# A convolution and two MLP layers on one core: the second product goes tile by tile in three banks, with the low parts of two chunks added up

## The chip, the cores and the metric

One NeuronCore of a Trainium2 chip runs the kernel; the other cores are idle. The metric is the device time of one execution in microseconds (us), lower is better. Three runs of the kernel before gave 2135.5, 2136.12 and 2136.22 us, median 2136.12.

## What is computed

Three stages follow each other on 16384 tokens of width 192, all in float32:

```
w   = softmax(weight, axis=-1)              # 8 heads x 7 taps
y   = causal convolution of x over 7 tokens, head h (24 columns) with taps w[h]
h   = y @ w_in1   (192 -> 2048);  g = max(h, 0)**2;       z   = g @ w_out1   (2048 -> 192)
h   = z @ w_in2   (192 -> 2048);  g = max(0.01*h, h);     out = g @ w_out2   (2048 -> 192)
```

The products run on TensorE in float32r, one pass each. To keep float32 accuracy every operand is split into a high part (rounded to float32r) and a low part (the rest), and three products are added: high by high, high weight by low data, low weight by high data.

## The kernel before, in words

**Tiles.** Tokens go in 32 tiles of 512 (`NT`, `TT`). The hidden width 2048 goes in 16 chunks of 128 (`NF`), two chunks to a step index p from 0 to 7 (`NP`). A *unit* is a tile in one of the two layers, l = 1 or 2; in what follows (l, t) names it. Two tiles make a pair q.

**Half arrays.** Every matmul uses 64 of the 128 rows of the array (`halves(0)` or `halves(1)`), and two of them, one on each half, run side by side. Such a couple is called a *slot* here. [...]

**First product.** `g1(u, p)` makes the two chunks of step p for one tile: 9 slots, into two of four banks `h`. Each item that this generator yields is one slot.

**Between the products.** ScalarE takes a chunk out of its bank with a ReLU (layer 1, line 531) or a leaky ReLU (layer 2, line 533) into `g`; in layer 1 it is squared, one chunk on ScalarE (line 540), the other on VectorE (line 538). `high` (line 558, ScalarE) rounds `g` to `hi`; `low` (line 562, VectorE) makes `lo = g - hi`. The tiles `g`, `hi` and `lo` come from pools of 4, 5 and 5 buffers.

**Second product.** `g2(u, f)` takes chunk f of both tiles of a pair: 10 slots, into four banks: `o0m` and `o1m` (128 output columns of each tile) and `o0r` and `o1r` (the 64 others; high by high and low weight by high data lie side by side in one matmul and are added later). In its middle the halves change banks. The change is guarded by a GpSimd no-op that waits for the last matmul of one half, and for which the first matmul of the other half waits; two slots of the next `g1` stand between (`AHEAD = 2`).

**Order of work.** A step of the main loop is one tile and one p: the tiles of a pair alternate, so a pair has 16 steps, and the phases are pairs 0 and 1 in layer 1, pairs 0 and 1 in layer 2, pairs 2 and 3 in layer 1, and so on. A step issues `g1` of its own chunks and `g2` of two steps before (`LAG = 2`), 9 + 10 = 19 slots. At the end of a pair `evac` (lines 694 to 703) empties the four banks before the next pair's second product begins, five slots of `g1` further on (`GAP = 5`). In the first 16 steps a hand-written table (`ROW`) orders ScalarE and VectorE, since the weights are decoded there; later a budget of VectorE time per step (`STEP = 4100`, in ns) decides how many *pieces* are put between: taps of the convolution (line 390), 32x32 transposes (lines 366, 720), splits of the next operand (lines 430, 439), decoding of the weights.

**Four phases of 16 steps** make the steady cycle: one pair of a layer has 16 steps, two pairs per layer, two layers.

Of the kernel before, what the change touches and what calls it, by code (L numbers as in the profile page):

```python
# [20 lines left out]
STEP = 4100  # L21
DEBT = -4000
# [4 lines left out]
SECOND, THIRD = 16, 40  # L27
LEAD_W = 2
# [3 lines left out]
XB = 4  # L32
# [17 lines left out]
    "ybpdwLAyBdpapwThrp",  # L50
    "ldppABabhlp",
    "AyBydpabhdww",
    "lyAdappLhplBdwp",
    "pAbpapyhBprbywd",
# [6 lines left out]
def conv_moe_moe2_kernel(  # L61
# [46 lines left out]
    NM = NI + 2 * P  # L108
    W, WR = {}, {}

    def place(l, p):
        if (l, p) not in W:
            z = const.tile([P, 2 * NW], F32R, tag=f"w{l}{p}", name=f"w{l}")
            W[l, p] = z[:, 0:2 * NM].rearrange("p (a w) -> p a w", a=2)
            WR[l, p] = z[:, 2 * NM:].rearrange("p (c w) -> p c w", c=2)
        return W[l, p], WR[l, p]

    def lent(p, dtype=I32):

        return const.tile([P, 2 * NW], dtype, tag=f"w2{p}", name="lent")  # L120
# [3 lines left out]

    def weights_in(l, v, p, a, k):
        return W[l, p][v, a, P * k:P * k + P]

    def weights_out(l, v, f, what):
        p, c = divmod(f, 2)
        z, n = W[l, p][v], NI + P * c  # L130
        if what in ("m", "ml"):
            return z[:, len(what) - 1, n:n + P]
        return WR[l, p][v, c, 0:2 * R if what == "r" else R]
# [6 lines left out]
    ring, turns = const.tile([P, 3, TT], F32, name="ring"), [0]  # L140

    def ring_tile():
        turns[0] += 1
        return ring[:, turns[0] % 3, :]

    def load_w(l, p, t):

        t4 = t[:, 0:NI].rearrange("p (k f) w -> p k (f w)", k=3)
# [6 lines left out]
        for c0, d0, n in ((NI, 0, P), (NM, P, R)):  # L155
            nc.sync.dma_start(  # L156
                out=t[:, c0:c0 + 2 * n].rearrange("p (c d) w -> p c (d w)", d=n), in_=src[:, :, 2 * d0:2 * (d0 + n)]
            )
# [18 lines left out]
    def decode(l, p, t, a, b):  # L177
# [4 lines left out]
        e = min(b, NM)  # L182
        z, r = place(l, p)
        parts = [(lambda z: z[:, 0:e - a], z[:, 0, a:e], z[:, 1, a:e])]
        if b == NW:
            parts.append((lambda z: z[:, NM - a:n].rearrange("p (c d) -> p c d", d=R), r[:, :, 0:R], r[:, :, R:2 * R]))
# [41 lines left out]

        def copy_high():
            for of, high, _ in parts:  # L230
                nc.scalar.copy(out=high, in_=f32(of(T["t"])))
            ready[l, p, 0] = True

        def sign():
# [4 lines left out]
            if l == 1 and p >= BY_DMA:  # L239
                for of, high, _ in parts:  # L240
                    nc.sync.dma_start(out=f32(high), in_=f32(of(T["t"])))
                ready[l, p, 0] = True
            else:
# [8 lines left out]
        def low_():  # L252
            assert not by_add or "added" in T
            ready[l, p, 1] = True
            for of, _, low in parts:
                nc.vector.scalar_tensor_tensor(  # L256
                    out=low, in0=of(T["r"]) if by_add else f32(of(lo_w)), scalar=2.0 ** -20, in1=f32(of(T["p"])), op0=ALU.mult, op1=ALU.mult
                )

        return [(one, mantissa), (two, rest)], [(one, exponent)], [(two, sign), (one, power), (two, low_)]  # L260


# [4 lines left out]
    def room(u):  # L267

        if len(order) < XB:
            return True  # L270
        return u in X or g1_left[order[len(order) - XB]] == 0

# [277 lines left out]
    def late_chunk(u, f):  # L550
        return u in [(2, t) for t in ordered] and f > NF - 4
# [12 lines left out]
    final = {}  # L564
    in_turn = mybir.DependencyInfo(mybir.DependencyClass.Sync, mybir.DependencyReason.DATA)

    def g2(u, f):
# [3 lines left out]
        if f == 0:  # L571
            ops[u] = {(i, n): ps_o.tile([P, TT], F32, tag=f"o{i}{n}", name=f"o{i}{n}") for i in range(2) for n in "mr"}
# [7 lines left out]
        for part in range(2):  # L580
            side = part ^ (f % 2)
            for j, (n, c, z) in enumerate(main + rest):
                begin = f == 0 and part == 0 and j in (0, 3)
                end_ = f == NF - 1 and part == 1 and j in (2, 4)
                for half in range(2):
# [5 lines left out]
                    final[i, n] = ins  # L591
# [7 lines left out]

    def g2_last(u):  # L600


        l, q = u
        o = ops[u]
        F = range(NF - 4, NF)
        a = {(i, f): hi.pop(((l, 2 * q + i), f)) for i in range(2) for f in F}
        b = {(i, f): lo.pop(((l, 2 * q + i), f)) for i in range(2) for f in F}

        def of(i, n, chunks, closing=False):
            for f in chunks:  # L610
                kinds = [("m", a), ("ml", a), ("m", b)] if n == "m" else [("r", a), ("rh", b)]
                if closing and f == F[-1]:
                    kinds.reverse()
                for c, z in kinds:
                    yield i, n, f, c, z[i, f]

        plan = [
            [of(0, "r", F[:2]), of(1, "r", F[:2]), of(0, "r", F[2:]), of(1, "m", F[:1]), of(1, "r", F[2:]), of(1, "m", F[1:]),
             of(0, "m", F)],
            [of(1, "m", F[:1]), of(0, "m", F), of(0, "r", F, True), of(1, "r", F, True), of(1, "m", F[1:])],  # L620
        ]
        side = (NF - 5) % 2 ^ 1
        owner = {}
        for half in range(2):
            owner[side ^ half, "m"] = owner[1 - (side ^ half), "r"] = half
        by = {k: final.get(k) for k in owner}
        seq = [[x for y in z for x in y] for z in plan]
        left = {k: sum(x[:2] == k for z in seq for x in z) for k in owner}
        for pair in zip(*seq):
            for half, (i, n, f, c, z) in enumerate(pair):  # L630
                k = i, n
                left[k] -= 1
                rows = R if c == "rh" else P
                v = halves(half)
                ins = product(o[k][0:rows], weights_out(l, v, f, c), z[v], False, left[k] == 0).ins
                if owner[k] != half:
                    done = nc.gpsimd.nop(nofuse=True).ins
                    tc.add_manual_dep(done, by[k].name, in_turn, reason="halves take turns on a bank")
                    tc.add_manual_dep(ins, done.name, in_turn, reason="halves take turns on a bank")
                owner[k], by[k] = half, ins  # L640

    def evac_last(u):
        l, q = u
        o = ops.pop(u)
        z = ring_tile()
        t = f32(stage.tile([P, NW], I32, tag="m", name="zs")[:, 0:TT])
        y = stage.tile([P, 3, TT], F32, tag="w", name="y", bufs=2)
        dmas = [nc.sync, nc.scalar]

        def store(j, n, d0, i):  # L650
            r0 = (2 * q + i) * TT
            dmas[j % 2].dma_start(
                out=out[r0:r0 + TT, d0:d0 + 32].rearrange("(i t) d -> t i d", t=32),
                in_=y[32 * j:32 * j + 32, n].rearrange("p (i d) -> p i d", d=32),
            )

        for i in range(2):
            nc.scalar.copy(out=t[halves(i)], in_=o[i, "r"][halves(1 - i)])
        for i in range(2):
            v = halves(i)  # L660
            nc.vector.tensor_add(out=z[v], in0=o[i, "r"][v], in1=t[v])
            nc.vector.transpose(out=y[v, 2], in_=z[v])
            for j in range(2):
                store(2 * i + j, 2, P + 32 * j, i)
        nc.vector.transpose(out=y[:, 0], in_=o[0, "m"])
        c = f32(spare_tile())
        turned = [ps_h.tile([P, 2, P], F32, tag="h", name="turned") for _ in range(2)]
        for i in range(2):
            tokens = slice(2 * P * i, 2 * P * (i + 1))
            nc.scalar.copy(out=c[:, tokens], in_=o[1, "m"][:, tokens])  # L670
            for k in range(2):
                w = c[:, P * (2 * i + k):P * (2 * i + k + 1)]
                nc.tensor.matmul(out=turned[i][:, k, :], lhsT=w, rhs=ident, start=True, stop=True)
        for j in range(4):
            store(j, 0, 32 * j, 0)
        for i in range(2):
            w = y[:, 1, 2 * P * i:2 * P * (i + 1)]
            nc.vector.tensor_copy(out=w, in_=turned[i].rearrange("p k d -> p (k d)"))
            r0 = (2 * q + 1) * TT + 2 * P * i
            dmas[i].dma_start(  # L680
                out=out[r0:r0 + 2 * P, 0:P].rearrange("(k t) d -> t k d", t=P),
                in_=w.rearrange("p (k d) -> p k d", d=P),
            )

    def evac(u):

        l, q = u
        o = ops.pop(u)
        T = [2 * q, 2 * q + 1]
        z = {}  # L690

        def take(i):
            z[i] = ring_tile()
            (nc.vector.tensor_copy if i else nc.scalar.copy)(out=z[i], in_=o[i, "m"])

        def shift(i):
            if i == 0:
                z["s"], z["r"] = f32(stage.tile([P, NW], I32, tag="m", name="zs")[:, 0:TT]), ring_tile()
# [16 lines left out]
        y = {}  # L715

        def turn(n, src):
            if not y:
# [426 lines left out]
```

## Time and profile before

| what | value |
|---|---|
| median of the runs | 2136.12 us |
| span of the profiled execution | 2134.3 us (the runs' median lies 1.8 us above it) |
| TensorE busy | 2126.8 us, 100% of the span, 19512 matmul records |
| VectorE busy | 1328.9 us, 62% |
| ScalarE busy | 1417.1 us, 66% |
| GpSimd busy | 12.4 us, 1% |
| granted TensorE clock | 0.9 or more of full speed in all 40 slices |

How to read it: TensorE is never idle for long after the start, so what counts on it is the number of slots and the time of one. The busy shares of VectorE and ScalarE are means over two layers of different load. An engine that is idle a third of the time still sets when an operand is ready, because each engine runs its queue in order.

### The profile page before, as it was taken

Reading aid. Unit: us, or ns where it says so; the run is one execution under the profiler, and the core shown is the slowest. Engines: PE = TensorE matmul, PEld = TensorE weight load, DVE = VectorE, ACT = ScalarE, POOL = GpSimd, SP = SyncE. Lnnn points to the kernel's source line nnn. Section 1 sums busy time; section 2 is a strip of 40 time slices with the busy share of each in tenths; the row PEclk is TensorE's granted clock in tenths of the full one; section 3 lists DMA queues with packets and bytes.
Section 4 is the critical chain, followed back from the end, with each engine's and each line's share of the span. In section 5 each row is a group of like instructions: output and inputs, shape, how many; then the busy total and the mean of one; then the engine's idle time right before and its main releaser. Section 6 shows DMA issues by size and latency. Waiting matters only on the chain.

```text
span 2134.3 us, 46985 instructions
## 1 busy us (share of the span) xinstructions
PE 2126.8 (100%) x19512; PEld 2042.4 (96%) x19512; DVE 1328.9 (62%) x2083; ACT 1417.1 (66%) x2599; POOL 12.4 (1%) x34
## 2 busy tenths in 40 slices
PE   9999999999999999999999999999999999999999
PEld 6999999999999999999999999999999999999998
DVE  8986686546865368653686536954468544685433
ACT  7986567655676557765577655776557765577654
POOL 1000000000000000000000000000000000000000
PEclk9999999999999999999999999999999999999999
DMA  8631133011330112301223002231023210321101
GB/s 192 160 90 36 14 56 61 18 36 16 56 66 11 36 29 44 74 11 26 43 32 72 16 21 46 34 68 26 11 48 50 49 36 3 59 45 32 31 5 27
DMA packets 233005, 95.06 MB, mean 45 GB/s; under 512 B 204184, under 2 KB 219032, under 8 KB 232792
## 3 DMA queue, kind: packets, MB, share of 16 engines
q1 hardware_dynamic: 227512, 88.70, 21.2%
q0 software_dynamic: 1168, 2.75, 0.7%
q8 instruction: 152, 2.49, 0.5%
q10 hardware_dynamic: 4112, 0.62, 0.2%
q14 instruction: 61, 0.50, 0.1%
HBM read 25.19 MB, written 12.58 MB: 18 GB/s over the span
## 4 chain that ended last, share of the span: by engine, by line
PE 97%; DVE 1%; DMA 1%; SPq 0%; ACT 0%; issue 0%; ACTq 0%; DVEq 0%
PE h L499 46%; PE o1m L499 15%; PE o0m L499 15%; PE o0r L499 10%; PE o1r L499 10%; DMA raw_a<-in_x_dram 0%; DVE lo L562 0%; DVE acc_b L390 0%; DMA w_all<-in_weight_dram 0%; DVE w L256 0%; SPq L346 0%; SPq L156 0%; DMA raw_b<-in_x_dram 0%; DVE x L435 0%; ACT hi L558 0%
## 5 line engine op out<-in xcount | busy, mean ns | idle before, releaser
L499 PE MATMUL h<-x,w 64*128 64x512 f32 x9216 | 1216.4, 376 | 0.5 <-DVE x L435 0.5
L562 DVE TENSOR_TENSOR lo<-g,hi 128x512 fp32r<-128x512 f32 x1018 | 675.4, 689 | 748.0 <-ACT hi L558 664.6
L499 PEld LDWEIGHTS h<-x,w 64*128 64x128 f32 x9216 | 1021.0, 186 | 28.7 <-DVE x L435 0.9
L558 ACT CAST hi<-g 128x512 fp32r<-128x512 f32 x1016 | 600.0, 616 | 26.1 <-DVE g L538 17.5
L499 PE MATMUL o1m<-hi,w 64*128 64x512 f32 x2036 | 602.9, 376 | 0.0
L499 PE MATMUL o0m<-hi,w 64*128 64x512 f32 x2036 | 602.5, 376 | 0.0
L533 ACT ACTIVATE g<-h 128x512 f32<-128x512 f32 x512 | 305.6, 597 | 420.7 <-PE h L499 418.5
L531 ACT ACTIVATE g<-h 128x512 f32<-128x512 f32 x512 | 302.9, 594 | 227.9 <-PE h L499 227.3
L499 PE MATMUL o1m<-lo,w 64*128 64x512 f32 x1018 | 383.3, 376 | 1.0 <-DVE lo L562 0.9
L499 PE MATMUL o1r<-hi,w 64*128 64x512 f32 x1018 | 383.2, 376 | 0.0
L499 PE MATMUL o0m<-lo,w 64*128 64x512 f32 x1018 | 382.9, 376 | 0.0
L499 PE MATMUL o0r<-hi,w 64*128 64x512 f32 x1018 | 382.8, 376 | 0.0
L499 PE MATMUL o1r<-lo,w 64*64 64x512 f32 x1018 | 382.8, 376 | 0.0
L499 PE MATMUL o0r<-lo,w 64*64 64x512 f32 x1018 | 382.8, 376 | 0.0
L499 PEld LDWEIGHTS o0m<-hi,w 64*128 64x128 f32 x2036 | 354.9, 185 | 19.5
L499 PEld LDWEIGHTS o1m<-hi,w 64*128 64x128 f32 x2036 | 354.8, 185 | 19.6
L499 PEld LDWEIGHTS o1m<-lo,w 64*128 64x128 f32 x1018 | 189.3, 186 | 2.6 <-DVE lo L562 2.6
L499 PEld LDWEIGHTS o1r<-hi,w 64*128 64x128 f32 x1018 | 189.3, 186 | 1.0 <-issue 0.2
L499 PEld LDWEIGHTS o0r<-hi,w 64*128 64x128 f32 x1018 | 189.3, 186 | 0.8
L499 PEld LDWEIGHTS o0m<-lo,w 64*128 64x128 f32 x1018 | 189.3, 186 | 0.2
L540 ACT ACTIVATE g<-g 128x512 f32<-128x512 f32 x269 | 168.2, 628 | 0.2
L538 DVE TENSOR_TENSOR g<-g 128x512 f32<-128x512 f32 x243 | 166.4, 685 | 0.5
(115 smaller groups left out, 1065.5 us busy)
## 6 DMA issues: line engine op xcount, KB each, us to landing
x<-x SPq DMA_DIRECT2D x189, 256.0 KB
out_dram<-y SPq DMA_DIRECT2D x184, 64.0 KB
raw_a<-in_x_dram SPq DMA_DIRECT2D x127, 64.0 KB
raw_b<-in_x_dram SPq DMA_DIRECT2D x62, 64.0 KB
lent<-in_moe_w_out_dram SPq DMA_DIRECT2D x13, 256.0 KB
lent<-in_moe_w_in_dram SPq DMA_DIRECT2D x13, 192.0 KB
lent<-in_moe_w_in_dram SPq DMA_DIRECT2D x13, 128.0 KB
lent<-in_moe_w_out_dram SPq DMA_DIRECT2D x13, 128.0 KB
```

The source lines that it names most:

```text
L499: return nc.tensor.matmul(out=o.rearrange("p (b a) -> p b a", a=2), lhsT=w, rhs=z.rearrange("p (a b) -> p b a", a=2), start=begin, stop=end_,)
L531: nc.scalar.activation(out=g, in_=hps.pop((u, f)), func=ACTF.Relu)
L533: nc.scalar.activation(out=g, in_=hps.pop((u, f)), func=ACTF.Prelu, alpha=0.01)
L538: nc.vector.tensor_mul(out=g, in0=g, in1=g)
L540: nc.scalar.activation(out=g, in_=g, func=ACTF.Square)
L558: nc.scalar.copy(out=a, in_=gsp[u, f])
L562: nc.vector.tensor_sub(out=b, in0=gsp.pop((u, f)), in1=f32(hi[u, f]))
```

## The change

The second product now takes one tile at a time, in **three banks**, and all 16 chunks of a tile are done before the next tile begins. Units go one by one, (1,t), (1,t+1), (2,t), (2,t+1), eight steps each; only pair 0 still runs as a pair. So tile changes come every 8 steps. A step still has `g1` of its own chunks (9 slots), now cut in 5 + 2 + 2, and the second product of the step before the last, in three groups of three slots (`g2_one`, `paired`, `COVER = 2`), one after each cut. The three banks of a tile are called M, F and E below, as in `evac_one`: M holds 128 columns by half the array, F and E the others, and E is finished after the second group of the last step, M and F after the third. Four bank tags are handed round, so a new tile has one bank free and takes over E, then F, then (one tile on) M.

From step 48 on (`THREE = 48`) VectorE also **adds the low parts** of the two chunks of a step (`add_low`, line 619 of the changed file, tile `both`), and GpSimd makes **differences of weight columns** (`differences`: one copy and two subtractions, 128x64 each, per layer and p, once) such that one matmul with `both` and two with a single low part and a difference take the place of matmuls on each low part: 9 slots instead of 10. Emptying a tile (`evac_one`): `early` copies E twice (ScalarE, lines 743, 744), `other` copies a half of F (ScalarE, 747), `add_rest` reads F (VectorE, 750), `add_main` reads M (VectorE, 753). `SHORT = 3880` replaces `STEP` in the budget from step 48 on. The weights lie in another layout, for which GpSimd copies two blocks of 64 columns per layer and p (`repeats`). Operand tiles go from four buffers to three.

The core of the diff (the layout of the weights, the last unit, stores and the table are left out):

```diff
-XB = 4
+XB = 3
+THREE = 48
+COVER = 2
...
+    def differences(l, p):
+        z = W[l, p]
+        nc.gpsimd.tensor_copy(out=z[:, BH1:BH1 + R], in_=f32(z[:, A1 + R:A1 + P]))
+        for to, x, y in ((DA, A1, AH0), (DC, CH0, CH1)):
+            nc.gpsimd.tensor_tensor(out=z[:, to:to + R], in0=f32(z[:, x:x + R]), in1=f32(z[:, y:y + R]), op=ALU.subtract)
...
+    def add_low(u, p):
...
+        nc.vector.tensor_add(out=c, in0=f32(lo[u, 2 * p]), in1=f32(lo[u, 2 * p + 1]))
...
+    def chain_of(u, p):
...
+        G, L = (2, 1) if t % 2 == 0 else (1, 2)
+        of = {0: [("m", 0, a[0]), ("m", 1, a[1])], G: [("g", 0, a[0]), ("g", 1, a[1])], L: [("l", 0, a[0]), ("l", 1, a[1])]}
+        if c is not None:
+            of[G].append(("d", 0, b[0]))
+            of[0].append(("d", 1, b[1]))
+            of[L].append(("s", 0, c))
+        else:
+            of[0] += [("m", 0, b[0]), ("m", 1, b[1])]
+            of[L][1:1] = [("rh", 0, b[0]), ("rh", 1, b[1])]
...
+    def g2_one(u, p):
+        if p == 0:
+            ops[u] = [new_bank() for _ in range(3)]
+        of = chain_of(u, p)
+        turn = ((0, 1, 2), (1, 2, 0)) if p % 2 == 0 else ((2, 1, 0), (0, 2, 1))
...
+            else:
+                z = g2_one(u2, p2)
+                advance(going, going[1] - 2 * COVER)
+                run(z, 1)
+                advance(going, COVER)
+                run(z, 1)
+                advance(going)
+                run(z)
+                if p2 == NP - 1:
+                    alone = True
+                    leaving, then = evac_one(u2)
...
+                one, two = (Z, A) if l == 1 else (A, Z)
+                act(*one)
+                act(*two)
+                needed(s, 10000)
+                if not (alone and dec):
+                    pieces(s, left, 700)
+                if l == 1:
+                    square(*Z, vector)
+                    square(*A, False)
+                if alone:
+                    leaving[1]()
+                    leaving[2]()
+                pieces(s, left)
...
+                high(*one)
+                high(*two)
+                low(*one)
+                low(*two)
+                if three:
+                    add_low(u, p)
+                if alone:
+                    leaving[3]()
```

**TensorE's queue.** In the steady part of the kernel before, layer 1, half of a step's second product and the slots around it (`h` is the first product, `w_...` a weight buffer; a row with x4 stands for four matmuls, two slots):

```order
L499 MATMUL o1m<-hi,w_222 128x512 [waits Pool_sequencer_49]
L499 MATMUL o0m<-hi,w_222 128x512
L499 MATMUL o1m<-hi,w_222 128x512
L499 MATMUL o0m<-hi,w_222 128x512
L499 MATMUL o1m<-lo,w_222 128x512
L499 MATMUL o0m<-lo,w_222 128x512
L499 MATMUL o0r<-hi,w_222 128x512
L499 MATMUL o1r<-hi,w_222 128x512
L499 MATMUL o0r<-lo,w_222 64x512
L499 MATMUL o1r<-lo,w_222 64x512
L499 MATMUL h<-x,w_251 128x512 x4
```

And the first two groups of a tile's first step in the changed kernel, in layer 1; `o0r` is the bank E and `o1m` the bank F of the tile before:

```order
L544 MATMUL o0r<-hi,w_222 128x512 [waits PE_49,Activation_49]
L544 MATMUL o1r<-hi,w_222 128x512
L544 MATMUL o0r<-hi,w_222 128x512
L544 MATMUL o1r<-lo,w_222 128x512 [waits DVE_49]
L544 MATMUL o0r<-lo,w_222 128x512 [waits DVE_49]
L544 MATMUL h<-x,w_311 128x512 x4
L544 MATMUL o0r<-hi,w_222 128x512 [waits Pool_sequencer_49]
L544 MATMUL o1m<-hi,w_222 128x512 [waits DVE_49]
L544 MATMUL o0r<-hi,w_222 128x512
L544 MATMUL o1m<-hi,w_222 128x512
L544 MATMUL o0r<-lo,w_222 128x512
L544 MATMUL o1m<-both,w_222 128x512
```

Ten matmuls between two pieces of `g1` have become six, twice there is a hand-over through GpSimd in a step instead of once, and the second group waits for VectorE's `add_rest`. In all 10240 matmuls into the banks `o` have become 9312.

**VectorE's queue**, two steps of layer 1 with a tile change, before (`g<-g` is the square, 390 a tap, 694 to 703 `evac`, 720 a transpose of the output):

```order
L562 TENSOR_TENSOR lo<-g,hi 128x512 [waits PE_49,Activation_49] x2
L694 COPY ring<-o1m 128x512 [waits PE_49]
L703 TENSOR_TENSOR ring<-o0r,zs 64x512 [waits Activation_49]
L703 TENSOR_TENSOR ring<-o1r,zs 64x512 [waits Activation_49]
L538 TENSOR_TENSOR g<-g 128x512
L720 STREAM_TRANSPOSE y<-ring 128x512
L562 TENSOR_TENSOR lo<-g,hi 128x512 [waits Activation_49] x2
L538 TENSOR_TENSOR g<-g 128x512 [waits Activation_49]
```

and in the changed kernel, the second and third step of (1,t) with t even (583 is the square, 607 `low`, 435 a tap, 763 a transpose of the output):

```order
L435 SCALAR_TENSOR_TENSOR acc_b<-xT_b,taps,acc_b 128x512
L583 TENSOR_TENSOR g<-g 128x512 [waits Activation_49]
L750 TENSOR_TENSOR ring<-o0r,zs 64x512 [waits Activation_49]
L435 SCALAR_TENSOR_TENSOR acc_b<-xT_b,taps,acc_b 128x512 [waits DVE_49] x2
L607 TENSOR_TENSOR lo<-g,hi 128x512 [waits Activation_49] x2
L619 TENSOR_TENSOR both<-lo 128x512 [waits DVE_49]
L753 TENSOR_TENSOR ring<-o1r,ring 128x512
L763 STREAM_TRANSPOSE y<-ring 128x512 [waits DVE_49]
L583 TENSOR_TENSOR g<-g 128x512 [waits Activation_49]
L607 TENSOR_TENSOR lo<-g,hi 128x512 [waits Activation_49]
L607 TENSOR_TENSOR lo<-g,hi 128x512 [waits PE_49,Activation_49]
L619 TENSOR_TENSOR both<-lo 128x512 [waits DVE_49]
```

The square, the two low parts and the sum of a step now stand in one run at its end, and the square of the same step stands before its own low parts; before, the two chunks of a step were one step apart.

## Rows read from the trace of the kernel before

**Rows 1.** The page, part 1: busy time of each engine.

```profile
span 2134.3 us, 46985 instructions
...
PE 2126.8 (100%) x19512; PEld 2042.4 (96%) x19512; DVE 1328.9 (62%) x2083; ACT 1417.1 (66%) x2599; POOL 12.4 (1%) x34
```

**Rows 2.** Busy time by stretch: two of the start, then layer 1, layer 2.

```profile
core 0: us, PE busy (x) PEld busy (x) DVE busy (x) ACT busy (x) POOL busy (x), PEclk, DMA share, GB/s
18.66:98.80 80.14, 78.67 (x666) 69.01 (x667) 75.69 (x122) 72.55 (x127) 8.11 (x9) 1.00 0.84 197
98.80:164.46 65.66, 65.66 (x611) 62.67 (x609) 58.93 (x88) 54.62 (x100) 0.00 (x0) 1.00 0.28 73
...
820.62:951.85 131.23, 131.23 (x1220) 127.26 (x1218) 85.90 (x134) 95.44 (x174) 0.00 (x0) 1.00 0.19 35
951.85:1083.08 131.23, 131.23 (x1219) 127.25 (x1218) 73.41 (x118) 76.48 (x144) 0.00 (x0) 1.00 0.22 39
```

**Rows 3.** The chain that ended last: start us, us; two pair changes.

```profile
820.62 2.59 PE h L499 x24
886.24 2.59 PE h L499 x24
```

**Rows 4.** Groups by form: busy us, mean ns | idle before.

```profile
L562 DVE TENSOR_TENSOR lo<-g,hi 128x512 fp32r<-128x512 f32 x1018 | 675.4, 689 | 748.0 <-ACT hi L558 664.6 <-PE o1r L499 48.9 <-PE o0r L499 32.1
...
L885 POOL MEMSET idle<- 128x512 f32 x1 | 0.5, 525 | 0.0
```

**Rows 5.** Timeline of TensorE at a hand-over of banks: start us, us.

```profile
1003.27 0.38 PE L499 MATMUL o0r<-lo,w 64*64 64x512 f32 x1
1003.43 0.65 PE L499 MATMUL h<-x,w 64*128 64x512 f32 x4
...
1003.75 0.18 PEld L499 LDWEIGHTS o1m<-hi,w 64*128 64x128 f32 x1
...
1003.86 0.38 PE L499 MATMUL o1m<-hi,w 64*128 64x512 f32 x1
```

**Rows 6.** Timeline of VectorE in layer 1: start us, us, [idle before].

```profile
822.62 0.69 DVE L703 TENSOR_TENSOR ring<-o1r,zs 64x512 f32<-64x512 f32 x1
823.35 0.69 DVE L538 TENSOR_TENSOR g<-g 128x512 f32<-128x512 f32 x1
...
824.72 0.69 DVE L562 TENSOR_TENSOR lo<-g,hi 128x512 fp32r<-128x512 f32 x1
...
830.96 0.16 DVE L365 COPY xT_a<-xT_a 128x6 f32<-128x6 f32 x1
831.16 0.71 DVE L366 STREAM_TRANSPOSE xT_a<-raw_a 128x512 f32<-128x512 f32 x1
831.79 0.67 DVE L720 STREAM_TRANSPOSE y<-ring 128x512 f32<-128x512 f32 x1
...
832.75 1.29 DVE L562 TENSOR_TENSOR lo<-g,hi 128x512 fp32r<-128x512 f32 x2
833.95 0.68 DVE L538 TENSOR_TENSOR g<-g 128x512 f32<-128x512 f32 x1
834.55 2.32 DVE L390 SCALAR_TENSOR_TENSOR acc_a<-xT_a,taps,acc_a 128x512 f32<-128x512 f32 x3
836.79 1.29 DVE L562 TENSOR_TENSOR lo<-g,hi 128x512 fp32r<-128x512 f32 x2
```

**Rows 7.** Timeline of ScalarE in layer 1: start us, us, [idle before].

```profile
821.29 0.58 ACT L699 COPY zs<-o0r 64x512 f32<-64x512 f32 x1
821.90 0.58 ACT L699 COPY zs<-o1r 64x512 f32<-64x512 f32 x1
822.50 0.60 ACT L531 ACTIVATE g<-h 128x512 f32<-128x512 f32 x1
824.07 0.62 ACT L558 CAST hi<-g 128x512 fp32r<-128x512 f32 x1 [0.98 <-DVE g L538]
824.60 0.62 ACT L540 ACTIVATE g<-g 128x512 f32<-128x512 f32 x1
...
838.51 0.60 ACT L531 ACTIVATE g<-h 128x512 f32<-128x512 f32 x1 [1.32 <-PE h L499]
839.01 0.61 ACT L558 CAST hi<-g 128x512 fp32r<-128x512 f32 x1
```

**Rows 8.** Waits: who waited for whom: us in total, times, longest.

```profile
POOL ring L209 <- DVE g L538: 9.5, 1, 9.5
```

**Rows 9.** Timeline of the end: last matmul into a bank, last VectorE instruction.

```profile
2128.20 0.38 PE L499 MATMUL o1m<-spare,w 64*128 64x512 f32 x1
...
2130.47 0.87 DVE L678 COPY y<-turned 128x256 f32<-128x256 f32 x2 [1.01 <-PE turned L673]
```

More of the change, by code (lines that the diff above doesn't have):

```diff
@@ L227, in exponent, with made @@
             on_scalar(lambda: nc.scalar.activation(out=T["t"], in_=T["t"], func=ACTF.Relu, scale=8.0, bias=bias_e))
+        def made(what):
+            T[what] = True
+            if a == 0 and "low" in T and "high" in T:
+                repeats(l, p)
         def copy_high():
-            for of, high, _ in parts:
-                nc.scalar.copy(out=high, in_=f32(of(T["t"])))
+            for of, to in highs:
+                nc.scalar.copy(out=to, in_=f32(of(T["t"])))
             ready[l, p, 0] = True
+            made("high")
         def sign():
@@ L597, in g2 @@
             yield
-    def g2_last(u):
[L603 to L640, printed above, removed]
@@ new lines, in paired @@
+    def paired(u, seqs, fresh, closing):
+        l, t = u
+        o = [z for z, _ in ops[u]]
+        left = {k: sum(x[0] == k for z in seqs for x in z) for k in range(3)}
+        used, start = {}, 0
+        assert len(seqs[0]) == len(seqs[1])
+        for j, pair in enumerate(zip(*seqs)):
+            assert pair[0][0] != pair[1][0]
+            if any(used.get((pair[h][0], 1 - h), -9) >= max(start, j - 2) for h in range(2)):
+                yield
+                start = j
+            for half, (k, f, what, z) in enumerate(pair):
+                used[k, half] = j
+                left[k] -= 1
+                assert ready.get((l, f // 2, 0)) and ready.get((l, f // 2, 1))
+                v = halves(half)
+                rows = R if what == "rh" else P
+                begin = fresh and (u, k) not in holder
+                ins = product(o[k][0:rows], weights_out(l, v, f, what), z[v], begin, closing and left[k] == 0).ins
+                if holder.get((u, k), half) != half:
+                    done = nc.gpsimd.nop(nofuse=True).ins
+                    tc.add_manual_dep(done, lastly[u, k].name, in_turn, reason="halves take turns on a bank")
+                    tc.add_manual_dep(ins, done.name, in_turn, reason="halves take turns on a bank")
+                holder[u, k], lastly[u, k] = half, ins
+        yield
@@ L775, in fill_dec @@
         def fill_dec():
-            parts = [(0, 0, NI), (0, NI, NW)] + [(n, 0, NW) for n in range(1, len(loads))]
+            parts = [(0, NO, NW), (0, 0, NO)] + [(n, 0, NW) for n in range(1, len(loads))]
             got = {}
@@ L825, in fill_dec @@
                 done += dec[k][1]
+            for l, s0 in ((2, THREE - 2), (1, first_use[1, 4] - 4)):
+                for p in range(NP):
+                    gate = lambda at=s0 + p: now[0] >= at
+                    dec.append((s0 + p, 0, lambda l=l, p=p: differences(l, p), gate, s0 + p + 2))
         budget = [0]
@@ L1080, in conv_moe_moe2_kernel @@
                 continue
[L1081 to L1095 removed]
+            if leaving:
+                while leave:
+                    z = leave.popleft()
+                    z[2]()
+                    release()
+                    budget[0] -= max(z[1], 0)
+                while dec and getattr(dec[0][2], "second", False):
+                    decode_one()
+                if alone:
+                    leaving[0]()
@@ L1096, in conv_moe_moe2_kernel @@
+            if leaving and not alone:
                 for c, fn in leaving:
@@ L1112, in conv_moe_moe2_kernel @@
         release()
[L1113 removed]
+        run(g2_last(steps[-1][0]))
         evac_last(steps[-1][0])
```

427 lines of the change are left out of this document (260 added, 167 removed).

## The prediction

> **What bounds the kernel now.** I read the busy times first: TensorE 2126.8 of 2134.3 us, VectorE 62%, ScalarE 66% [rows 1]. Then the stretches: a layer's two pairs take 131.23 us in either layer, and TensorE is busy in all of it, while VectorE has 85.90 us of work in layer 1 and 73.41 in layer 2 [rows 2]. The chain gives the unit of the sum: from one pair change to the next 886.24 - 820.62 = 65.62 us [rows 3] for 16 steps of 19 slots, so a slot takes 65.62/304 = 0.2158 us and a step 4.10. Pair changes cost TensorE nothing. [...]
>
> **Slots removed.** 10240 matmuls into the banks `o` become 9312: 928 fewer are 464 slots, one per step from step 48 on, -464 x 0.2158 = **-100.1 us**. A step then has 18 slots, 3.885 us.
>
> **What VectorE gets.** The 464 sums `both` are forms like `low`, 0.69 us [rows 4]. In layer 2 a step needs two low parts, a sum and about one piece, some 2.6 of 3.885 us: hidden. Layer 1 has to be walked through, because the order in the queue counts, not the sum of work. The spacings from start to start are: 0.60 us behind an instruction that the next doesn't depend on (833.95 to 834.55); 0.63 behind a transpose; 0.785 from tap to dependent tap, (2.32 - 0.75)/2, which leaves 2.24 - 1.57 = 0.67 from a tap to another kind; 0.72 behind a read of PSUM, or where the next needs the result (0.69 and 0.03) [rows 6]. From VectorE's square over ScalarE's `hi` to the low part it is 823.35 to 824.07 to 824.72, or 1.37 us [rows 6, 7], and in the new order nothing else may fill that gap but pieces that stand behind the square.
>
> A layer-1 step with one piece ahead of its square (and at most one behind it) therefore takes VectorE 0.60 + 0.67 + 1.37 + 0.60 + 0.72 = 3.96 us, more than TensorE's 3.885. Two steps are worse. I take as time 0 the start of a cycle of 32 steps, step 0 being the first of (1,t), t even; step k begins on TensorE at 3.885k. A step's last `g1` slot starts 14 slots in and ends 0.38 later [rows 5], at 3.40.
> - Step 1 (tile change): E is final 12 slots and 0.38 us into the step, at 6.86; two copies at 0.60 [rows 7]; the ReLUs at 8.08 and 8.58 (0.50 apart [rows 7]); square 8.71; `add_rest` 9.31; two taps 10.03 and 10.82; low parts 11.49 and 12.09; `both` starts at 12.81.
> - Step 2: `add_main`, transpose, square: 0.60 + 0.72 + 0.63, then 1.37 + 0.60 + 0.72: `both` at 17.45.
> - Step 3 (transpose first) 3.92: 21.37; step 4 3.96: 25.33; step 5 (a small copy 0.20, a transpose 0.63): 29.45; steps 6 to 8, 3.96 each: 41.33.
> - Step 9 (tile change): tap 41.93, square 42.60, `add_rest` 43.20 to 43.89.
>
> TensorE needs these. At a hand-over a matmul starts 0.2 us after the end of what it waits for (1003.27 + 0.38 = 1003.65, next at 1003.86 [rows 5]); I take that for all releases. For t even and p even `both` is wanted two steps later 7 slots in, for p odd 5 slots later, which suffices. Step 2's ends at 17.45 + 0.69: start 18.34 against 4 x 3.885 + 1.51 = 17.05, a wait of 1.29 so far. Step 4's: 26.22 against 24.82, 1.40; step 6's: 34.30 against 32.59, 1.71. Bank F is wanted 10 slots into step 10, at 41.01, and VectorE lets go of it for 44.09: **3.08 us** in all. Afterwards VectorE has one short piece or none per step (3.33 with none) and catches up. Thirteen cycles are full: **+40.0 us**. In the fourteenth nothing is prepared any more; there only ScalarE's late `other` holds F at its two layer-1 changes. By step 1: the square on ScalarE at 9.20, `other` 0.52 later, ended at 10.30, start 10.50 against 7.77 + 2.16 = 9.93, 0.57 each, **+1.1 us**.
>
> Bounds of this term: 0 if the gap were filled, and, if every layer-2 change waited too, what the second rival gives. I stay with the walk, as each spacing has its row.
>
> [...]
>
> **ScalarE.** A layer-1 step has two ReLUs, a square and two casts, by rows 7 0.5 to 0.65 us apart, about 2.7 us, and six copies per 16 steps instead of three: hidden in 3.885, apart from their places above.
>
> **GpSimd.** No row shows a 128x64 copy or subtraction; the nearest is a 128x512 memset of 0.525 us [rows 4]. `differences` has three in a batch, 16 batches, one per step: at most 1.6 us. They wait for nothing late, and queue between the last hand-over of a step (slot 13) and the first of the next (slot 8), 13 slots or 2.8 us. So 0; without that cover 16 x 1.6 = 25 us. `repeats` comes in the decoding: the next hand-over stands behind a wait for decoded weights, and GpSimd's longest wait for VectorE there was 9.5 us [rows 8].
>
> **Start and end.** Steps 18 to 33 are full of decoding (VectorE 58.93 of 65.66 us [rows 2]) and now change tiles three times, in the old count of slots. From below 0; from above one such wait of 9.5 and three changes of 0.9, 12 us. I take 5, nearer to the tile changes, since the start already has its waits (78.67 busy of 80.14 [rows 2]). At the end copies, transposes and stores follow the last matmul as before (6.1 us from 2128.20 [rows 9]); the last tile passes two more dependent instructions and fewer transposes: +1, between -1 and 2. Fewer buffers for operands cost nothing: their splits stand several steps ahead.
>
> **Sum.** 2134.3 - 100.1 + 40.0 + 1.1 + 5 + 1 = 2081.3 us of span; the median of the runs lies 1.8 above the profiled span: **2083 us**.
>
> **The rivals.**
> - *No waits in layer 1.* If VectorE keeps up, say because the round trip over ScalarE hides, the sum is 2134.3 - 100.1 + 5 + 1 + 1.8 = 2042 us. For it: the old kernel ran layer 1 with steps of 4.04 on VectorE (832.75 to 836.79 [rows 6]) and never waited. Against: there the gap was filled, and the 3.96 isn't. Chance 0.20.
> - *Layer-2 changes wait too.* By the same walk, in a layer-2 step: E final at 2.97, two copies, ReLUs at 4.17 and 4.67, `other` 5.18 to 5.76, which is 1.88 into the next step; with the 0.2 of a release 2.08, and F is wanted at 2.16. One cast more ahead of it (0.6) at the 28 layer-2 changes gives +17: 2100 us. Chance 0.14.
> - [...] Chance 0.03. [...]
> - *Slower: the second hand-over is not covered.* A step now changes halves twice in mid-step, and two slots stand between each time. If the second cost TensorE a slot, 464 x 0.2158 = 100 us come back: 2183. It decides from (2136 - 2083)/464 = 0.115 us per step. For it: the weights of the next matmul load 0.10 us after the old half ends, so the cover is thin. Against: that matmul still starts in its slot (1003.43 to 1003.86, two slots [rows 5]), and the distance stays two slots. Chance 0.05.
>
> **How the numbers follow.** The forecast has the remaining 0.58, with 2068 to 2098 as its own range (spacings off by 1% move a cycle by 0.4 us, the start 0 to 12). The range of 8 in 10 takes in the first rival and most of the second: 2040 to 2102. It leaves out 0.08 for the last two and some 0.1 at the edges. Under 0.2% (4 us) a run can't tell from no change. Faster by more: all but the last rival, 0.95; that one's smaller sizes give 0.01 for same; slower 0.04.
>
> **What would show it.** In layer 2 a step of 3.885 us, and TensorE never idle. A cycle of 32 steps takes 127.4 us (32 x 3.885 = 124.3, and 3.1) instead of 131.2. TensorE's weight loads wait for `both` (line 619) and, at changes within layer 1, for line 750; ScalarE's `hi` in layer 1 is what VectorE's idle time ends on. VectorE is over 80% busy. I am wrong if cycles take 124.3 (no waits), if weight loads wait for GpSimd at each step, or if the clock falls below 1.00 where TensorE waits.

## The result, and the profile after

The changed kernel takes 2162.23 us (median of 4 runs, 2161.25 to 2162.54), against 2136.17 us for the kernel before in the same session. The ratio is 1.0122, with a 95% interval of 1.0108 to 1.0137: **slower by 26 us**, where 2083 us was predicted and 0.04 given to slower. The sign is wrong, and by 79 us.

The profile's page after, part 1 and the first line of part 4 (the chain that ended last, by engine):

```profile
span 2160.8 us, 47005 instructions
...
PE 2084.4 (96%) x18592; PEld 1974.9 (91%) x18592; DVE 1648.7 (76%) x2575; ACT 1478.4 (68%) x2700; POOL 60.1 (3%) x114
...
PE 65%; DVE 17%; ACT 11%; issue 5%; DMA 1%; SPq 0%; DVEq 0%; ACTq 0%
```

TensorE did lose 920 matmul records and 42 us of busy time [rows 1], but it now stands still for 76 us in place of 7.5, and 28% of the chain is VectorE and ScalarE. Three stretches of the start, then one cycle of 32 steps, from its second step on, layer 1 and layer 2 (roughly), in the form of [rows 2]:

```profile
core 0: us, PE busy (x) PEld busy (x) DVE busy (x) ACT busy (x) POOL busy (x), PEclk, DMA share, GB/s
100.00:110.00 10.00, 6.74 (x49) 5.71 (x47) 9.09 (x15) 7.82 (x15) 4.57 (x2) 0.86 0.00 0
140.00:150.00 10.00, 6.65 (x43) 5.25 (x41) 7.49 (x13) 5.83 (x10) 0.68 (x2) 0.74 0.79 202
250.00:260.00 10.00, 8.28 (x58) 7.54 (x56) 5.84 (x9) 4.99 (x9) 1.29 (x5) 0.83 0.16 29
712.03:779.48 67.45, 64.26 (x579) 60.96 (x578) 54.72 (x86) 48.38 (x88) 0.00 (x0) 1.00 0.12 21
779.48:843.23 63.75, 63.14 (x579) 61.16 (x578) 47.03 (x75) 41.52 (x78) 0.00 (x0) 1.00 0.28 55
```

The cycle takes 843.23 - 712.03 = **131.20 us**, as before (131.23), where 18 slots a step are 32 x 18 x 0.2158 = 124.3 and 127.4 was predicted. What the 32 removed slots give, the waits take. And in the start the granted clock falls below 1.00 in stretches in which TensorE waited; before, it was 1.00 [rows 2].

Who waited for whom (us in total, times, longest):

```profile
DVE lo L607 <- ACT hi L603: 289.7, 304, 3.2
...
ACT hi L603 <- DVE g L583: 130.8, 97, 3.6
...
DVE ring L750 <- ACT ring L747: 94.2, 60, 3.9
...
PEld o1m L544 <- DVE ring L750: 37.7, 30, 2.8
...
PEld o0r L544 <- DVE ring L750: 26.2, 28, 1.3
...
PEld o1m L544 <- DVE both L619: 16.8, 25, 1.0
```

TensorE waits most for line 750, `add_rest`, at all 58 tile changes among single tiles; and line 750 itself waited for line 747, `other`, at each of the 60 places where it stands. One such change in layer 1, from the timelines of ScalarE, VectorE and TensorE (start us, us, [idle before <-releaser]); the last line is the first ReLU 32 steps later:

```profile
711.43 0.58 ACT L744 COPY zs<-o1m 64x512 f32<-64x512 f32 x1
712.03 1.08 ACT L576 ACTIVATE g<-h 128x512 f32<-128x512 f32 x2
713.15 0.63 ACT L585 ACTIVATE g<-g 128x512 f32<-128x512 f32 x1
713.81 0.58 ACT L747 COPY ring<-o0r 64x512 f32<-64x512 f32 x1
...
712.67 0.69 DVE L583 TENSOR_TENSOR g<-g 128x512 f32<-128x512 f32 x1
714.42 0.69 DVE L750 TENSOR_TENSOR ring<-o0r,zs 64x512 f32<-64x512 f32 x1 [1.06 <-ACT ring L747]
...
715.17 0.48 PE L544 MATMUL o0r<-hi,w 64*128 64x512 f32 x1 [0.97 <-DVE ring L750]
...
843.23 1.08 ACT L576 ACTIVATE g<-h 128x512 f32<-128x512 f32 x2
```

`add_rest` had its operand at 712.01 (`zs`) and VectorE was free at 713.36; it began at 714.42, when `other` ended. Both read bank F, and the program lets them do so only in the order in which they are issued: the change's order shows a wait for ScalarE at line 750, and its releaser in the trace is line 747. Both also write the tile `ring`, in different thirds of it, but that isn't what is guarded: in the kernel before, VectorE wrote one third of `ring` while ScalarE still wrote another, from two different banks, at all 30 pair changes, as here:

```profile
820.69 0.58 ACT L694 COPY ring<-o0m 128x512 f32<-128x512 f32 x1
821.08 0.69 DVE L694 COPY ring<-o1m 128x512 f32<-128x512 f32 x1
```

So bank F comes free 3.08 us behind the first ReLU, with both reads one after the other and ScalarE's square ahead of them. The program has the two read different halves of the partitions. No run here shows the two reads at once; whether that wait could be left out wasn't tried.

Where the 26.4 us of span come from, by the start of each step's first ReLU against the kernel before:

| stretch | predicted | measured |
|---|---|---|
| to step 48 | +5 | +20.0 |
| steps 48 to 64 | -3.5 | +3.7 |
| 13 cycles of 32 steps | 13 x -3.83 = -49.7 | +0.3 |
| steps 480 to 511 | -5.8 | -1.5 |
| end | +1 | +3.9 |
| sum | -53 | +26.4 |

### The profile page after: what moved, and what is told of

Its sections match the earlier page's. It is cut to its first block, busy times and chain, and to the rows that moved or that the text cites. A ratio compares the mean times of both kernels' runs of the same rounds, so it can differ in the third digit from the quotient of the medians.

```text
span 2160.8 us, 47005 instructions
## 1 busy us (share of the span) xinstructions
PE 2084.4 (96%) x18592; PEld 1974.9 (91%) x18592; DVE 1648.7 (76%) x2575; ACT 1478.4 (68%) x2700; POOL 60.1 (3%) x114
## 4 chain that ended last, share of the span: by engine, by line
PE 65%; DVE 17%; ACT 11%; issue 5%; DMA 1%; SPq 0%; DVEq 0%; ACTq 0%
PE h L544 31%; PE o1m L544 12%; PE o0r L544 11%; PE o1r L544 7%; DVE lo L607 5%; PE o0m L544 4%; ACT hi L603 2%; DVE g L583 2%; DVE acc_b L435 2%; DVE ring L750 2%; ACT g L576 2%; DVE acc_a L435 2%; ACT ring L747 2%; ACT zs L744 2%; ACT g L578 2%
## 5 line engine op out<-in xcount | busy, mean ns | idle before, releaser
L607 DVE TENSOR_TENSOR lo<-g,hi 128x512 fp32r<-128x512 f32 x1022 | 661.8, 688 | 347.1 <-ACT hi L603 289.7
L544 PE MATMUL o0r<-hi,w 64*128 64x512 f32 x1948 | 601.6, 384 | 17.9 <-DVE ring L750 17.9
L544 PE MATMUL o0r<-lo,w 64*128 64x512 f32 (+1 forms) x1022 | 383.5, 378 | 0.4 <-DVE lo L607 0.4
L544 PE MATMUL o1m<-both,w 64*128 64x512 f32 x926 | 352.4, 381 | 8.1 <-DVE both L619 8.1
L619 DVE TENSOR_TENSOR both<-lo 128x512 fp32r<-128x512 f32 x463 | 320.5, 692 | 18.0
L544 PE MATMUL o0m<-hi,w 64*128 64x512 f32 x1088 | 326.9, 380 | 4.4 <-ACT ring L835 3.2
L544 PE MATMUL o0m<-lo,w 64*128 64x512 f32 x560 | 209.1, 378 | 0.6 <-DVE lo L607 0.5
L544 PEld LDWEIGHTS o0m<-hi,w 64*128 64x128 f32 x1088 | 191.2, 186 | 9.7 <-ACT ring L835 4.0
L544 PE MATMUL o1r<-lo,w 64*128 64x512 f32 (+1 forms) x526 | 198.0, 376 | 0.0
L544 PEld LDWEIGHTS o1m<-both,w 64*128 64x128 f32 x926 | 172.3, 186 | 19.0 <-DVE both L619 16.8
L544 PEld LDWEIGHTS o0r<-lo,w 64*128 64x128 f32 (+1 forms) x1022 | 187.4, 183 | 2.3 <-issue 0.8
## 6 DMA issues: line engine op xcount, KB each, us to landing
lent<-in_moe_w_in_dram SPq DMA_DIRECT2D x13, 128.0 KB
lent<-in_moe_w_out_dram SPq DMA_DIRECT2D x13, 128.0 KB
```

The source lines that it names most:

```text
L544: return nc.tensor.matmul(out=o.rearrange("p (b a) -> p b a", a=2), lhsT=w, rhs=z.rearrange("p (a b) -> p b a", a=2), start=begin, stop=end_,)
L607: nc.vector.tensor_sub(out=b, in0=gsp.pop((u, f)), in1=f32(hi[u, f]))
L619: nc.vector.tensor_add(out=c, in0=f32(lo[u, 2 * p]), in1=f32(lo[u, 2 * p + 1]))
```

## The experiments

Three theories for the cycle and the start, and a rival: (1) at a tile change bank F comes free late, since `add_rest` stands behind `other`; (2) VectorE's layer-1 step with its round trip over ScalarE is the limit; (3) the start loses its time to banks and tiles that come free late at the first changes; (4) the rival: GpSimd's queue is held up by `repeats`. "Cycle" is the distance of the ReLU starts over 32 steps, in the steady part.

**add_rest first**, right behind `early` and ahead of the squares (in `evac_last` too it goes ahead of `other`).

```diff
                 if alone:
                     leaving[0]()
+                    leaving[2]()
...
                 if alone:
                     leaving[1]()
-                    leaving[2]()
```

> add_rest (VectorE) is issued right behind early, ahead of the squares, so that other (ScalarE) reads bank F after it. Theory 1 (the program lets the two engines read bank F only one after the other; in the changed kernel add_rest stood idle 1.06 us until other was done, at 713.36 to 714.42, and F came free at 715.11): F now comes free with other, at about 714.4 of the same cycle, 0.7 us earlier at each of the four tile changes of a cycle, and VectorE no longer loses the idle 1.06 us, so that `both` of step 4 comes up to 1 us earlier. Cycle 131.2 -> 127.5 to 128.5 us, time 2115 to 2130 us. Rival (VectorE's own order sets the end, whoever reads first): other now waits for add_rest as long as add_rest waited for other; cycle 131 us, time 2155 to 2165 us.

Measured: 2116.95 us, 0.9911 of the kernel before (0.9896 to 0.9926), cycle 128.0. At a layer-1 change:

```profile
861.77 0.58 ACT L744 COPY zs<-o0r 64x512 f32<-64x512 f32 x1
862.38 1.08 ACT L576 ACTIVATE g<-h 128x512 f32<-128x512 f32 x2
863.49 0.63 ACT L585 ACTIVATE g<-g 128x512 f32<-128x512 f32 x1
864.15 0.58 ACT L747 COPY ring<-o1m 64x512 f32<-64x512 f32 x1
...
862.60 0.68 DVE L750 TENSOR_TENSOR ring<-o1m,zs 64x512 f32<-64x512 f32 x1
...
864.78 0.48 PE L544 MATMUL o1m<-hi,w 64*128 64x512 f32 x1 [0.88 <-ACT ring L747]
```

`add_rest` now runs during the ReLUs, and F comes free with `other` at 864.73, 2.35 us behind the first ReLU in place of 3.08. Moving one call up gives 45 us, and the kernel becomes faster than before the change. Theory 1 holds. At both layer-2 changes of a cycle the wait of 0.74 us is gone. The rival that `other` would wait as long instead is out: it had one wait of 0.8 us in the whole run.

**No `both`**, the tile-by-tile product alone (19 slots):

```diff
-THREE = 48
+THREE = 10 ** 6
...
-            for l, s0 in ((2, THREE - 2), (1, first_use[1, 4] - 4)):
+            for l, s0 in ():
```

> The tile-by-tile second product alone: no `both`, no differences, 19 slots a step throughout (step 4.10 us). Theory 1 (what costs are the tile changes with three banks: 1.40 + 2.28 + 0.74 + 0.74 us of waits for bank F and E in a cycle): the waits on F stay, only the 1.5 us for `both` at steps 4 to 8 go; cycle 131.2 + 4 to 5 us = 135 to 136 us, time 2136 + 13 x 4.5 + 20 to 25 at the start = 2210 to 2225 us. Rival (VectorE's 0.69 us more in every step is what makes bank F late): the waits go with `both`; cycle 131.2 to 132 us, time 2155 to 2170 us.

Measured: 2241.55 us, 1.0489 (1.0473 to 1.0505), cycle 136.60. By theory 1, and more (it gave 2210 to 2225 us): 5.4 us per cycle over the 131.23 of the kernel before, all in the steps around the four changes. Its waits for `add_rest` are no shorter without `both`:

```profile
DVE ring L750 <- ACT ring L747: 107.8, 60, 5.4
PEld o1m L544 <- DVE ring L750: 47.2, 30, 2.8
```

So going tile by tile costs 5.4 us a cycle, and `both` gives that back: its 32 slots (6.9 us) less 1.5. A step without a wait takes 4.10 us here and 3.89 in the change, so the removed slots were worth what the prediction said.

**All squares of layer 1 on ScalarE** (`vector = False`).

> All squares of layer 1 on ScalarE, none on VectorE. Theory 2 (VectorE's layer-1 step, with square, ScalarE's high and the low behind it, is the limit): VectorE has 0.69 us less to do in each of 16 steps of a cycle and `both` is no longer late at steps 4 to 8; cycle 131.2 -> 128.5 to 129.5 us, time 2125 to 2140 us. Theory 1 (add_rest behind other decides): the bank F waits stay; and ScalarE, with two ReLUs, two squares and two high parts at 0.54, 0.63 and 0.57 us (3.5 of the 3.885 us of a step) and three or four copies at a tile change, becomes late there: cycle 131 to 133 us, time 2160 to 2190 us.

Measured: 2144.60 us, 1.0039 (1.0024 to 1.0054), cycle 129.58. Steps 4 to 7 of a cycle, 3.96 to 4.12 us in the change, take 3.88 to 3.90; theory 2 has a share too, 17.6 us, though the step at such a change takes 4.88 in place of 4.50, as ScalarE comes to `other` later. The time lies above theory 2's range (2125 to 2140), so it isn't the whole.

**High parts in the order A, Z**, which takes out only the round trip:

```diff
-                high(*one)
-                high(*two)
-                low(*one)
-                low(*two)
+                high(*A)
+                high(*Z)
+                low(*A)
+                low(*Z)
```

> Only the order of the high and low parts in layer 1: first those of the chunk that ScalarE squares itself (A), then those of the chunk that VectorE squares (Z); nothing added or left out. In the changed kernel the high part of Z stands first and waits for VectorE's square, which stands behind a convolution tap: ScalarE idle 1.2 us and VectorE 0.7 us before the low parts in most layer-1 steps. Theory 2 (that round trip makes the layer-1 step 3.97 us where 18 slots take 3.885, and makes `both` late behind a tile change): steps 4 to 10 of a cycle lose up to 2 us less; cycle 131.2 -> 129 to 130 us, time 2130 to 2147 us. Rival (only add_rest behind other counts): the waits on bank F stay as they are; cycle 131 us, time 2157 to 2163 us.

Measured: 2138.49 us, 1.0013 (1.0004 to 1.0023), cycle 129.41: 23.7 us from an order alone. How a layer-1 step looks with Z first (ScalarE and VectorE, from the kernel with `add_rest` first):

```profile
843.29 0.68 DVE L583 TENSOR_TENSOR g<-g 128x512 f32<-128x512 f32 x1
844.66 1.29 DVE L607 TENSOR_TENSOR lo<-g,hi 128x512 fp32r<-128x512 f32 x2 [0.69 <-ACT hi L603]
...
844.01 1.14 ACT L603 CAST hi<-g 128x512 fp32r<-128x512 f32 x2 [1.18 <-DVE g L583]
```

and with A first (from the kernel with three edits, below):

```profile
841.71 0.68 DVE L583 TENSOR_TENSOR g<-g 128x512 f32<-128x512 f32 x1
842.53 1.29 DVE L607 TENSOR_TENSOR lo<-g,hi 128x512 fp32r<-128x512 f32 x2
...
841.88 1.22 ACT L603 CAST hi<-g 128x512 fp32r<-128x512 f32 x2
```

ScalarE rounds A while VectorE squares Z, and VectorE's 0.69 us of idle time ahead of the low parts shrinks to 842.53 - 842.39 = 0.14.

**add_rest first, and `other` ahead of ScalarE's square.**

```diff
                     square(*Z, vector)
-                    square(*A, False)
                 if alone:
                     leaving[1]()
+                if l == 1:
+                    square(*A, False)
```

> add_rest ahead of other, and other ahead of ScalarE's square; the high parts as in the changed kernel. With add_rest first, bank F of a layer-1 change still comes free with other, which stands behind a square of 0.63 us (square 863.49, other 864.15 to 864.73, and TensorE waited 0.88 us for it). If bank F decides still: 0.6 us less at steps 2 and 10 of each cycle, cycle 127.9 -> 126.7 to 127.3 us, time 2100 to 2110 us. If the order of the high parts holds it up instead: cycle 127.9 us, time 2114 to 2120 us, and the gain of the kernel with all three edits over this one is 33 us or more.

Measured: 2105.51 us, 0.9858 (0.9841 to 0.9874), cycle 127.33: 11.4 us more, as expected if bank F still decides.

**These and the order A, Z together.**

> add_rest ahead of other, other ahead of ScalarE's square, and the high parts in the order A, Z. If the two causes add up (cycle 127.9 us with add_rest first; the rest of it, 3.5 us over 18 slots a step, is 1.4 us at step 8, 1.0 at step 2, 0.7 at steps 0 and 1 and 0.45 at steps 4 to 7): steps 2 to 8 lose half, cycle 125.5 to 126.8 us, time 2085 to 2103 us. If the order of the high parts only matters behind a late bank F, which is gone with the first edit: cycle 127.5 to 128 us, time 2112 to 2118 us.

Measured: 2080.93 us, 0.9745 (0.9730 to 0.9759), cycle 125.58. In the cycle the parts add up: 3.87 us for bank F and 1.79 for the high parts, 5.66 expected, 5.62 measured. Of 6.9 us lost per cycle 1.3 are left. Beyond the low end of what was expected for the time (2085).

**`repeats` on VectorE** (`nc.gpsimd` becomes `nc.vector` in its two copies).

> The 16 copies of `repeats` on VectorE in place of GpSimd. Theory 4 (GpSimd's queue, where the no-ops and the copies of high parts by DMA stand, is held up at the start by `repeats`, which waited up to 18.3 us for decoded weights and took up to 4.39 us): steps 8 to 18 lose 3 to 6 us less; time 2154 to 2159 us. Theory 3 (the start's loss is banks that come free late and VectorE's and ScalarE's order): no change, or up to 3 us more as VectorE has 16 more operations before step 50; time 2160 to 2166 us. The cycle stays 131.2 us by both.

Measured: 2172.07 us, 1.0168 (1.0151 to 1.0185), slower than the change by 10 us, beyond what either theory gave. By step 8 it stands 7.5 us behind the kernel before, the change 0.5, and nothing is won back by step 18 (18.6 against 10.8). The waits that theory 4 is about do go: in the change VectorE's low parts waited 4.3 us, and TensorE's weight loads 1.4, for high parts that GpSimd's queue sends by DMA, and here neither waits for one. But the start isn't shorter for it, so theory 4's forecast falls. As the edit loads VectorE in the same stretch, a share of GpSimd in the start isn't ruled out; that VectorE's longer queue is what costs there is argued, not shown.

**The pair's banks let go earlier** (steps 17 and 49).

```diff
                 act(*one)
                 act(*two)
+                if leaving and not alone:
+                    for c, fn in leaving:
+                        fn()
+                        budget[0] -= c
...
-                while leaving and not alone and dec and getattr(dec[0][2], "second", False):
-                    decode_one()
...
-            if leaving and not alone:
+            if leaving and not alone and u in in_pair:
```

> At the two places where a pair of tiles is let go while a single tile is under way (steps 17 and 49) the copies out of the pair's banks are issued right behind the two ReLUs, ahead of the square, the high and the low parts. Theory (those banks come free late because three ScalarE operations of 0.6 us stand ahead; steps 17/18 lost 7 us and step 49/50 4.9 us against the kernel before, part of it with a granted clock of 0.83 to 0.86 behind the wait): 1.8 us earlier at each place and less of the slow clock, 4 to 8 us in all, time 2154 to 2158 us. Rival (the loss there is decoding's, which gives the staging tile late): within 2 us of the changed kernel, 2160 to 2164 us. The high and low parts of that step come 2.3 us later, which can take back what is won.

Measured: 2163.10 us, 1.0129 (1.0112 to 1.0146): nothing. But step 51 starts 9.9 us earlier than in the change, and step 68 only 2.0: the gain was made and lost again, 7.2 us of it in step 59, at whose end VectorE's transpose into the tile `y` waits 7.1 us.

**The pair's banks let go earlier and `repeats` on VectorE, on top of the three edits:**

> The same with the pair's banks let go ahead of the square at steps 17 and 49, and `repeats` on VectorE. The pair's banks alone brought step 51 9.9 us earlier, but by step 68 all but 2 us of that was lost again at one wait of 5.4 us at step 60 (VectorE's transpose waited 7.1 us for the tile y, whose outputs of the pair had not been stored). If the start's gain is kept only up to that wait: the time of the kernel without these two edits, within 3 us. If not: 5 to 10 us less than it.

Measured: 2083.11 us, 0.9755 (0.9740 to 0.9769), within 3 us of the kernel with three edits: it is 3.7 us ahead of that kernel at step 51 and 1.0 behind it at step 60.

**`repeats` back on GpSimd, and y's transpose due later:**

> The kernel with the three edits, with the pair's banks let go ahead of the square at steps 17 and 49, and the two transposes of the first single tile of layer 2 put off by three steps, so that they come after the pair's outputs are stored (with both edits of the start but not this one, TensorE stood still at 280 to 290, busy 3.68 of 10 us there). `repeats` stays on GpSimd. Theory 3 (banks late at the first changes, then one wait for the tile y): step 18 loses 1.5 us in place of 6, step 50 1.3 in place of 3.7, step 60 nothing in place of 3.7 to 8; time 2068 to 2074 us. Rival (a third wait stands behind these, as y did behind the banks): 2079 to 2084 us.

Measured: 2078.08 us, 0.9731 (0.9716 to 0.9745), outside what either theory gave. This edit missed its aim: the transpose's due time was put off, but work is taken ahead of its due time where there is budget, and the transpose stayed where it was. So the run shows the wait instead (VectorE, TensorE; then TensorE's stretches):

```profile
286.67 0.71 DVE L763 STREAM_TRANSPOSE y<-ring 128x512 f32<-128x512 f32 x1 [8.53 <-DMA x<-x]
...
288.61 0.79 PE L544 MATMUL o1r<-lo,w 64*128 64x512 f32 x1 [6.31 <-DVE lo L607]
...
280.00:290.00 10.00, 3.69 (x28) 3.07 (x26) 3.26 (x6) 2.11 (x4) 0.00 (x0) 0.72 0.55 117
290.00:300.00 10.00, 10.00 (x74) 8.36 (x72) 6.09 (x10) 4.74 (x9) 2.09 (x6) 0.77 0.20 22
```

The releaser shown is a load of `x`; the same queue had issued the stores of the pair's outputs out of `y` from 254.27 to 281.34. That the transpose waits for those stores is read from this order; that the transpose is what holds TensorE up is what the next run tests.

**A gate for that transpose:**

```diff
-            then.append((700, main, None, None))
+            then.append((700, main, (lambda: now[0] >= 61) if t == 2 else None, None))
```

> As the kernel before it (three edits, the pair's banks let go early), but the first single tile's transpose into y now has a gate that holds it back to step 61; in that kernel only its due time had been put off, and as work is taken ahead of its due time it had stayed at step 58, where VectorE stood still 8.53 us (278.14 to 286.67) and TensorE 6.31 us, with a granted clock of 0.72 and 0.77 in the 20 us around. If y is what is late there, step 60 loses nothing in place of 8 us and the clock stays at 1.00 from 280 to 300: time 2068 to 2073 us. Rival (the loads and stores that share the transfers hold up something else at the same moment): a wait of several us stands elsewhere between steps 58 and 66, time 2075 to 2081 us.

Measured: 2069.51 us (5 runs, 2067.52 to 2071.89), **0.9688 (0.9675 to 0.9702)**, the fastest of all. Step 60 is 9.1 us behind the kernel before in place of 19.8, and no other wait has taken its place. The same two stretches, and the page:

```profile
280.00:290.00 10.00, 10.00 (x96) 9.69 (x94) 6.61 (x11) 5.29 (x11) 2.30 (x9) 1.00 0.79 155
290.00:300.00 10.00, 10.00 (x96) 9.85 (x94) 6.83 (x13) 6.30 (x13) 1.66 (x7) 1.00 0.25 32
...
span 2067.9 us, 46971 instructions
...
PE 2049.3 (99%) x18592; PEld 1964.3 (95%) x18592; DVE 1644.4 (80%) x2575; ACT 1499.3 (73%) x2700; POOL 55.2 (3%) x114
```

**The two edits of the start on the changed kernel alone:**

> The changed kernel with the two edits of the start alone: the pair's banks let go ahead of the square, the first single tile's transpose held back to step 61; add_rest, other and the high parts as in the change. If the start's loss and the cycle's loss are separate sums, this gains what both edits gained on top of the three others (2080.9 to 2069.5, 11.4 us): 2149 to 2153 us, and step 76 stands 14 to 18 us behind the kernel before instead of 27.6. If the late bank F behind other makes its own loss at the start as well, so that the y tile isn't reached earlier: 2157 to 2163 us.

Measured: 2155.17 us, 1.0094 (1.0076 to 1.0112), between the two expectations; step 76 stands 21.1 us behind. So the two edits gain 7.1 us here and 11.4 on top of the three others. That the start's loss and the late bank F overlap fits this, but where they do isn't shown: in step 25, at the start's first change among single tiles, this kernel loses 4.9 us and the one with all edits 1.0, yet the kernel without the gate, which has the same order up to there, loses 2.6.

## Why the prediction was wrong, point by point

- **Slots removed, -100.1 us: right.** A step without a wait takes 3.89 us in the change, and 3.88 to 3.90 with all edits. Without `both` a step is 4.10.
- **"Square 8.71; `add_rest` 9.31": the step that failed.** The walk placed `add_rest` as VectorE's queue has it, right behind the square, with `zs` as its only operand. It waits for `other`, whose end the walk itself, for the last cycle, put at 10.30. The wait was in the order shown (line 750 waits for ScalarE), and was read as the wait for `zs`. At the change shown it costs VectorE 1.06 us and bank F 0.7 us: 3.2 us a cycle and 45 us in all, by the first experiment. With `add_rest` ahead of `other`, as the walk had it in effect, the cycle takes 128.0 us, near the 127.4 predicted.
- **The round trip over ScalarE: right in its mechanism and size.** A step with one piece takes 3.97 us (predicted 3.96). What it costs, 1.79 us a cycle, was part of the predicted 3.08. That the order A, Z removes it without a new operation wasn't seen.
- **Layer-2 changes at 0: wrong; the rival's waits came, its reason didn't.** It gave 0.6 us to each of 28; measured 0.74 twice a cycle. That the size is near is luck: the reason is not one cast more ahead of `other`, but the same `add_rest` behind it, which the prediction's bank F in layer 2 left out: with `add_rest` first these waits are gone.
- **The start, 5 us out of 0 to 12: wrong; it was 20 by step 48.** The tile changes were priced at 0.9 us each; the first two took 6.9 and 6.6 us (steps 16 to 18, 24 to 26). The pair's banks are let go behind three more operations of ScalarE, and after the wait TensorE's granted clock is low (0.50 from 108.00 to 110.30 us), which the prediction named as a way to be wrong and gave no price. That the tile y, now a single buffer, is a floor under step 60 wasn't considered.
- **GpSimd at 0 in the steady part: right.** TensorE waits for no hand-over in the cycle, so the rival of 2183 us, the one slower case, named the wrong mechanism.
- **End +1: it was +3.9**; no run takes it apart.
- **No waits (2042 us): wrong too**, but the edits show how far it can be neared: 125.58 a cycle against 124.3.
- **The signs.** Weight loads waiting for `both` (16.8 us) and for line 750, and VectorE's idle time ending on `hi` (289.7 us), came as named; "VectorE over 80% busy" didn't (76%).
- **What decided the sign.** The 0.04 for slower rested on the second hand-over alone. Against the 100.1 us of removed slots the kernel loses 126.5. The late bank (45 us, 57 with the square ahead of `other`), the round trip (24) and the start (20) make 101 of them; the rest isn't told apart. With the late bank alone put right, the kernel is faster than the one before (0.9911).

## What to carry to other kernels

When a bank has two readers on two engines, find out whether the second waits for the first, and issue first the one whose operand is ready first; a wait shown without its releaser is to be followed to the instruction that ends it. Where two chunks are squared on two engines, let the engine that rounds begin with the one it has itself. In a start that is paced by several resources, freeing one shows only the next: read the distance step by step, since a gain of 10 us can be gone 17 steps later.

## What the runs showed of the hardware

The clock's fall at the start. Some of TensorE's matmuls behind the waits at steps 17 and 18 of the changed kernel:

```profile
106.44 0.48 PE L544 MATMUL o0m<-hi,w 64*128 64x512 f32 x1 [2.63 <-ACT ring L835]
107.55 0.76 PE L544 MATMUL o1m<-hi,w 64*128 64x512 f32 x1 [0.63 <-DVE ring L835]
...
108.11 0.63 PE L544 MATMUL o1m<-lo,w 64*64 64x512 f32 x1
108.54 0.63 PE L544 MATMUL o1m<-lo,w 64*64 64x512 f32 x1
108.96 0.63 PE L544 MATMUL o1m<-hi,w 64*128 64x512 f32 x1
...
110.92 0.38 PE L544 MATMUL o1m<-hi,w 64*128 64x512 f32 x1
```

A matmul takes 0.63 us there and 0.38 behind it, and a slot 0.43, twice 0.2158; the granted clock is 0.50 from 108.00 to 110.30. In these runs the length of the wait alone doesn't tell how long that lasts. In the kernel with three edits the waits there are shorter in sum (1.92 and 0.89 us), yet the clock of 100 to 110 is 0.66, in the change 0.86, and that step is no faster for it: it loses 5.9 us, in the change 4.5. In the kernel with all edits, where the pair's banks are let go early, it is 1.00 from 100 to 110. In the changed kernel's cycle, with single waits up to 1.6 us, it is 1.00 in both stretches shown above, 712.03 to 843.23.

At the layer-1 change shown, the bank's release reached TensorE in 0.06 us: `add_rest` ends at 714.42 + 0.69 = 715.11 and the matmul starts at 715.17; the prediction had taken 0.2 us. GpSimd's copies of 128x64 took 0.23 to 4.39 us in the changed kernel. And the first 16 steps, whose order is the same in all kernels but the two with `repeats` on VectorE, lose between 1.9 and 6.7 us by step 16 in one execution or another; what sets that was not found.
